# Decode attention beside a gated MLP on one core: masking moved to ScalarE, the gMLP in three pieces, four quarters summed without a fold

## The chip, the core and the metric

The kernel runs on one core of a Trainium2 chip. Five engines work side by side and meet through semaphores: TensorE (PE; its weight loads are the row PEld), VectorE (DVE), ScalarE (ACT), GpSimd (POOL) and SyncE (SP), which here only issues loads. Sixteen DMA engines move data between the chip's memory and the core's buffer. The metric is the device time of one launch in microseconds, as the median over runs; a profiled execution beside them gives the trace.

## The reference

Two blocks read the same normalized input and are added to it:

```python
xn = _layernorm(x, axis=-1)
return x + _A_ref(xn, A_k_cache, A_v_cache, A_wq, A_wo) + _B_ref(xn, B_w_in, B_w_sp, B_b_sp, B_w_out)
```

Block A is attention of one new position against a cache: batch 4, 32 heads, 4096 cached positions, head width 128, model width 640, all bf16.

```python
q = (x @ wq).reshape(B, Sq, Hq, Dh)          # one query per head
scores = einsum('bhqd,bhkd->bhqk', q, k) * Dh ** (-0.5)
p = _softmax(scores, axis=-1)
o = einsum('bhqk,bhkd->bhqd', p, v)
return o.reshape(B, Sq, Hq * Dh) @ wo
```

Block B is a small gated MLP (gMLP): `z = gelu(xn @ w_in)`, 1728 columns; its second half is layer-normalized, scaled by the single number `w_sp`, shifted by `b_sp`, and multiplied with the first half; the product goes through `w_out`.

K and V are 134 MB each, and every byte is used once.

## The kernel before

**Tiles.** The 32 heads are cut in 4 groups of 8, and with 4 batches that makes 16 tiles (`NT`), each 8 heads of one batch. In a tile, 16 partitions hold one head, and every partition holds 256 positions of 128 numbers. A K tile is 8 MB and a V tile as much, loaded in two halves (units). The ring in the core's buffer has five units: a pair for the K tile in work, a pair for the next, and a single one (`SOLO`); V halves take the places that K tiles and earlier V halves leave. The gMLP's weights lie in the single unit at the start.

**Loads.** All are issued from SyncE's queue, in the order of a plan made ahead (`plan_k`, `plan_v`, `load_wo`): K of tile i+2 after both V halves of tile i, and a slice of `wo` after tiles 0, 4 and 8. `pump()` issues the next load as soon as, in program order, the unit's holder is marked `used`; on the chip the queue then waits for the holder's last reader. The queue is in order: a load that waits for its place holds all behind it.

**One tile** (`for i in range(NT)`), its K in four quarters of 64 positions per partition:
- `product` (L495, VectorE): the quarter times the query, in place, 128x8192 bf16.
- `fold` (L504, VectorE): the upper 64 of each 128 products added to the lower 64.
- `sums` (L513, TensorE): 8 matmuls with the identity add the 64 columns up to 8 per position, into PSUM (`s_ps`, two buffers).
- `row_sums` (L527, VectorE) reduces the 8 to a score, one quarter behind: it comes after the next quarter's product.
- After the four: `lane_max` (L536 VectorE, L538 ScalarE, L540 TensorE), then `exps`: the maximum (L546, VectorE) and the exponential on ScalarE (L550), which gives `p`, 128x256 bf16.
- `deal` (L561): `p` is spread to `p_m`, where each position has 8 columns, one for each head, and all but the own head's are zeros (`hmask`). Two GpSimd instructions of 128x1024 for a tile; in the last tile one of the two is VectorE's. `p_m` has two buffers, for even and odd tiles.
- `blocks` (L575, TensorE): probabilities times V, 32 matmuls for each half. The first half of tile i-1 stands in tile i behind the sums of its first quarter, the second behind those of its third, followed by `gather` (L589 ScalarE, L593 TensorE). The last two tiles have an order of their own: in tile 14 the first half of 13 comes behind the fourth quarter, and in tile 15 four of these stages follow its quarters. Tile 14's `exps` and `deal` stand in tile 15 behind its first fold.

The order on TensorE, VectorE, ScalarE and SyncE is the program's own; GpSimd's and what stands before the loop is placed by a scheduler.

**The gMLP.** `gmlp_in` (L363): 70 matmuls behind the third quarter's sums of tile 0, into `zT`. `gmlp_out`, after tile 0's `exps` and `deal`: GELU on VectorE with tanh on ScalarE (L373 to L387), 14 matmuls for the layer norm's sums (L392), a chain of 1x4 and 1x8 instructions with a square root on ScalarE (L405 to L426), a broadcast matmul (L435, L439), three VectorE rows (L440 to L452) and the product with `w_out` (L456). Only then are the weights marked used and the second V half of tile 0, which takes their unit, may be issued. The two numbers `w_sp` and `b_sp` are loaded from ScalarE's queue at the start (L103, L104) and copied to fp32 on VectorE inside `gmlp_out` (L418, L420).

**After a group of four tiles**: sum of the exponentials (`group_den`, L617 on GpSimd, L624, L626), `group_norm`, `group_turn`, `group_pick` and the product with `wo` (`group_proj`, L671).

Of the kernel before, what the change touches and what calls it, by code (L numbers as in the profile page):

```python
# [20 lines left out]
def kernel(  # L21
# [14 lines left out]
    nc = tc.nc  # L36
# [316 lines left out]
    gm["ac"] = work.tile([1, 2 * Bsz], FP32, name="ac")  # L353
    gm["yT"] = work.tile([P, NFC, Bsz], BF16, name="yT")

    def gmlp_in():
        zT = gm["zT"] = ps_pv.tile([P, 2, NFC, Bsz], FP32, tag="pv", name="zT")
        for t in range(2):
            f1 = t * Fh + NFF * P
            w_t = w_in_sb[:, :, t * Fh : f1].rearrange("p c (f k) -> p c k f", k=NFF)  # L360
            for k in range(NFC):
                for c in range(DC):
# [6 lines left out]
                    )  # L369
    def gmlp_out():  # L370
        zT = gm["zT"]
# [15 lines left out]
        nc.vector.tensor_tensor(out=sq[:], in0=gz[:, 1, :, :], in1=gz[:, 1, :, :], op=ALU.mult)  # L387

        s_ps = ps_m.tile([1, 2 * Bsz], FP32, tag="m", name="ln_ps")
        for src, at in ((gz[:, 1, :, :], 0), (sq[:], Bsz)):  # L390
            for k in range(NFC):
# [6 lines left out]
                )  # L398
        st, ac = gm["st"], gm["ac"]
        mean_t = st[:, 0:Bsz]  # L400
# [15 lines left out]
        )  # L416
        wsp_t = work.tile([1, 1], FP32, name="wsp_t")
        nc.vector.tensor_copy(out=wsp_t[:], in_=wsp_bf[:])  # L418
        bsp_t = work.tile([1, 1], FP32, name="bsp_t")
        nc.vector.tensor_copy(out=bsp_t[:], in_=bsp_bf[:])  # L420
        nc.vector.reciprocal(out=rst_t, in_=rst_t)
# [71 lines left out]
    def product(i, q):  # L493
# [6 lines left out]
        )  # L500

    def fold(i, q):
        t = quarter(i, q)
        nc.vector.tensor_tensor(  # L504
            out=t[:, :, 0:HD2], in0=t[:, :, 0:HD2], in1=t[:, :, HD2:Dh], op=ALU.add
        )

    def sums(i, q):
        t = quarter(i, q)
        s = sums_ps[i, q] = ps_s.tile([P, QC, RW], FP32, name="s_ps")  # L510
        n = HD2 // RW
        for g in range(n):
            nc.tensor.matmul(  # L513
                out=s[:],
                lhsT=ident[:],
                rhs=t[:, :, g * RW : (g + 1) * RW],
                start=(g == 0),
                stop=(g == n - 1),
            )
        if q % 2:  # L520
            used.add(("k", i, q // 2))
            pump()
# [35 lines left out]

    def deal(i, part, engine):
        g0, g1 = part * UC // GC, (part + 1) * UC // GC  # L560
        engine.tensor_tensor(  # L561
            out=p_m[i % 2][:, g0:g1, :].rearrange("p g (c h) -> p g c h", h=HT),
            in0=probs[i][:, part * UC : (part + 1) * UC]
            .rearrange("p (g c) -> p g c", c=GC)[:, :, :, None]
            .to_broadcast([P, UC // GC, GC, HT]),
            in1=hmask_bf[:, None, None, :].to_broadcast([P, UC // GC, GC, HT]),
            op=ALU.mult,
        )
# [113 lines left out]
    with tc.manual_schedule(engines={E.PE, E.DVE, E.Activation, E.SP}):  # L682
# [3 lines left out]
        for i in range(NT):  # L686
            ends = i >= 1 and i % Bsz == 0
            late = i - 1 if i == LAST else None
            for q in range(NQ):
# [7 lines left out]
                if q == 0 and late is not None:  # L697
                    exps(late)
                    deal(late, 0, nc.gpsimd)
                    deal(late, 1, nc.gpsimd)  # L700
                sums(i, q)
                if i == 0 and q == 2:
                    gmlp_in()
                if i % Bsz == Bsz - 1 and q == 1 and i // Bsz + 1 < HG:
                    stage_q(i // Bsz + 1)
# [23 lines left out]
            if i != LAST - 1:  # L729
                row_sums(i, NQ - 1)  # L730
                lane_max(i)
                if ends:
                    group_pick(i // Bsz - 1)
                exps(i)
                deal(i, 0, nc.gpsimd)
                deal(i, 1, nc.vector if i == LAST else nc.gpsimd)
            if ends:
                group_proj(i // Bsz - 1)
            if i == 0:
                gmlp_out()  # L740
                used.add("w")
                pump()
        assert not loads
# [46 lines left out]
```

## Time and profile before

| | |
|---|---|
| runs, median (range), us | 672.07 (670.62 to 672.6) |
| the profiled execution, us | 668.78 |
| its span, us | 666.8 |
| PE, DVE, ACT, POOL busy, us | 313.4, 507.4, 34.3, 97.9 |
| product (L495), 64 rows, mean | 4.558 us |
| fold (L504), 64 rows, mean | 2.447 us |
| mask on GpSimd (L561), 31 rows, mean | 3.035 us |
| exp (L550), 16 rows, mean | 0.508 us |
| HBM read | 282.24 MB |

The span runs from the first to the last instruction of the program; the execution's own time has what lies around it. Busy times of different engines overlap. In a timeline row stand the start, the duration, engine, line and operation, the tile written and those read, and in brackets the idle time before it and what ended it. A row of SPq is SyncE's queue: "x2" merges two issues, with the time from the first's start to the second's end. A row of the waits has the waiting line, the one waited for, the sum, the count and the longest. In rows by stretches there are busy time and count for PE, PEld, DVE, ACT and POOL, the granted TensorE clock (1 is full), the share of the DMA engines' time, and GB/s.

### The profile page before, as it was taken

The page shows a single profiled execution, that of the slowest core. Times are in us where ns is not written, and L with a number is a line of the kernel's source. Part 1 is how long each engine was busy: PE and PEld are TensorE (multiplying, and loading weights), DVE is VectorE, ACT ScalarE, POOL GpSimd, SP SyncE. Part 2 cuts the span into 40 slices and gives each one's busy share as a digit, 9 for nine tenths or more (in the row PEclk, how much of TensorE's full clock was granted, in tenths as well). Part 3 has the DMA queues.
Part 4 walks back from the last instruction along what each step waited for, and adds up shares of the span by engine and source line. Part 5 has one row for each costly group of instructions (what it writes and reads, how often), then busy time and mean ns, then how long its engine had stood idle before and what let it go on. Part 6 is the DMA issues. An engine that isn't in the chain of part 4 may idle for free.

```text
span 666.8 us, 4747 instructions
## 1 busy us (share of the span) xinstructions
PE 313.4 (47%) x2033; PEld 127.2 (19%) x2033; DVE 507.4 (76%) x278; ACT 34.3 (5%) x82; POOL 97.9 (15%) x60
## 2 busy tenths in 40 slices
PE   0355461625544455453516545263553445535656
PEld 0113120211211112121212211121121111211223
DVE  2496986949595796977948499694958579799970
ACT  0002001000000000000000000000000000000000
POOL 2002002020200321302020050402010032120501
PEclk9755675777868577675767666777786756856786
DMA  9999899999999999999999999999999999999997
GB/s 376 438 451 408 361 448 436 437 413 468 412 432 447 409 448 416 462 430 415 442 420 450 423 417 460 419 440 421 453 417 429 449 421 374 440 411 436 410 424 288
DMA packets 9873, 282.56 MB, mean 424 GB/s; under 512 B 1040, under 2 KB 2428, under 8 KB 2812
## 3 DMA queue, kind: packets, MB, share of 16 engines
q1 hardware_dynamic: 9832, 282.25, 98.6%
q8 instruction: 16, 0.26, 0.1%
q14 instruction: 5, 0.04, 0.0%
q10 hardware_dynamic: 20, 0.01, 0.0%
HBM read 282.24 MB, written 0.01 MB: 423 GB/s over the span
## 4 chain that ended last, share of the span: by engine, by line
DMA 48%; DVE 34%; PE 17%; ACT 1%; issue 1%; SPq 0%; DVEq 0%; ACTq 0%
DMA ring<-in_A_k_cache_dram 41%; DVE ring L495 19%; DVE ring L504 11%; PE s_ps L513 10%; PE pv_acc L575 5%; DMA ring<-in_A_v_cache_dram 3%; DMA wo<-in_A_wo_dram 3%; DVE s_sb L527 2%; PE zT L363 1%; PE pv L593 0%; DVE gt L383 0%; PE max_ps L540 0%; DVE gz L386 0%; ACT pv_sb L589 0%; DVE m L536 0%
## 5 line engine op out<-in xcount | busy, mean ns | idle before, releaser
L495 DVE TENSOR_TENSOR ring<-ring,qbc 128x8192 bf16<-128x8192 bf16 x64 | 291.7, 4558 | 46.2 <-DMA ring<-in_A_k_cache_dram 46.2
L513 PE MATMUL s_ps<-ring,ident 128*128 128x512 bf16 x512 | 187.9, 533 | 284.0 <-DVE ring L504 284.0
L561 POOL TENSOR_TENSOR pm<-p,hmask_bf 128x1024 bf16<-128x1024 bf16 x31 | 93.5, 3035 | 548.6 <-ACT p L550 496.4
L504 DVE TENSOR_TENSOR ring<-ring 128x4096 bf16<-128x4096 bf16 x64 | 156.6, 2447 | 0.5
L513 PEld LDWEIGHTS <-ident 128*128 128x128 bf16 x512 | 63.9, 126 | 385.5 <-issue 320.0
L575 PE MATMUL pv_acc<-ring,pm 128*32 128x512 bf16 x1008 | 77.4, 462 | 0.9 <-DMA ring<-in_A_v_cache_dram 0.9
L527 DVE TENSOR_REDUCE s_sb<-s_ps 128x64 f32<-128x512 f32 x64 | 43.8, 684 | 43.3 <-PE s_ps L513 43.3
L575 PEld LDWEIGHTS <-pm 128*32 128x32 bf16 x1008 | 27.8, 114 | 58.4 <-issue 46.9
L589 ACT COPY pv_sb<-pv_acc 128x512 f32<-128x512 f32 x16 | 9.4, 586 | 364.4 <-PE pv_acc L575 364.4
L593 PE MATMUL pv<-sel,pv_sb 128*128 128x8 f32 x128 | 16.9, 259 | 11.9 <-ACT pv_sb L589 11.9
L626 DVE RECIPROCAL rden<-den 128x32 f32<-128x32 f32 x4 | 1.4, 358 | 26.1 <-PE den L624 26.1
L593 PEld LDWEIGHTS pv<-sel,pv_sb 128*128 128x128 f32 x128 | 15.5, 191 | 19.9 <-ACT pv_sb L589 19.9
L540 PE MATMUL max_ps<-lay,head_scale 128*128 128x16 f32 x32 | 7.0, 294 | 23.4 <-ACT lay L538 23.4
L538 ACT ACTIVATE lay<-lane_diag,m 128x16 f32<-128x16 f32 x16 | 4.9, 308 | 159.1 <-DVE m L536 159.1
L540 PEld LDWEIGHTS max_ps<-lay,head_scale 128*128 128x128 f32 x32 | 5.4, 211 | 30.6 <-ACT lay L538 30.6
L546 DVE TENSOR_REDUCE nb<-max_ps 128x1 f32<-128x16 f32 x16 | 2.8, 174 | 10.3 <-PE max_ps L540 10.1
L327 DVE CAST q_sb<-q_ps 128x512 bf16<-128x512 f32 x1 | 0.7, 692 | 12.9 <-PE q_ps L320 12.9
L320 PE MATMUL q_ps<-ring,xnT 128*32 128x512 bf16 x40 | 4.5, 630 | 10.6 <-DMA ring<-in_A_wq_dram 10.6
L550 ACT ACTIVATE p<-s_sb,nb 128x256 bf16<-128x256 f32 x16 | 8.1, 508 | 12.3 <-DVE nb L546 12.3
L536 DVE TENSOR_REDUCE m<-s_sb 128x1 f32<-128x256 f32 x16 | 6.7, 420 | 0.5
L631 DVE TENSOR_TENSOR o_n<-pv,rden 128x32 bf16<-128x32 f32 x4 | 0.7, 186 | 7.5 <-PE pv L605 7.5
L671 PE MATMUL out_ps<-wo,o_r 128*4 128x320 bf16 x48 | 6.0, 420 | 0.3 <-DVE o_r L658 0.2
(91 smaller groups left out, 72.2 us busy)
## 6 DMA issues: line engine op xcount, KB each, us to landing
ring<-in_A_v_cache_dram SPq DMA_DIRECT2D x31, 4096.0 KB, 30.8
ring<-in_A_k_cache_dram SPq DMA_DIRECT2D x2, 4096.0 KB, 34.0
ring<-in_A_wq_dram SPq DMA_DIRECT2D x1, 5120.0 KB, 15.6
wo<-in_A_wo_dram SPq DMA_DIRECT2D x3, 1280.0 KB, 16.9
ring<-in_B_w_in_dram SPq DMA_DIRECT2D x1, 2160.0 KB, 38.1
ring<-in_A_v_cache_dram SPq DMA_DIRECT2D x1, 2048.0 KB
ring<-in_A_v_cache_dram SPq DMA_DIRECT2D x1, 1024.0 KB
ring<-in_A_v_cache_dram SPq DMA_DIRECT2D x2, 512.0 KB, 25.8
```

The source lines that it names most:

```text
L363: nc.tensor.matmul(out=zT[: P if k < NFF else FT, t, k, :], lhsT=w_t[:, c, k, :] if k < NFF else w_in_sb[:, c, f1 : f1 + FT], rhs=xnT[:, c ...
L495: nc.vector.tensor_tensor(out=t, in0=t, in1=qbcs[i // Bsz][:, i % Bsz, None, :].to_broadcast([P, QC, Dh]), op=ALU.mult,)
L504: nc.vector.tensor_tensor(out=t[:, :, 0:HD2], in0=t[:, :, 0:HD2], in1=t[:, :, HD2:Dh], op=ALU.add)
L513: nc.tensor.matmul(out=s[:], lhsT=ident[:], rhs=t[:, :, g * RW : (g + 1) * RW], start=(g == 0), stop=(g == n - 1),)
L527: nc.vector.tensor_reduce(out=scores[i][:, q * QC : (q + 1) * QC], in_=sums_ps.pop((i, q))[:], axis=AX.X, op=ALU.add,)
L536: nc.vector.tensor_reduce(out=m1[:], in_=scores[i][:], axis=AX.X, op=ALU.max)
L540: nc.tensor.matmul(out=ps[:], lhsT=head_scale[:], rhs=d[:], start=True, stop=True)
L550: nc.scalar.activation(out=p[:], in_=scores.pop(i)[:], func=ACT.Exp, bias=nb[:], scale=scale_qk, accum_out=acc[hg % NACC][:, b : b + 1],)
L561: engine.tensor_tensor(out=p_m[i % 2][:, g0:g1, :].rearrange("p g (c h) -> p g c h", h=HT), in0=probs[i][:, part * UC : (part + 1) * UC] . ...
L575: nc.tensor.matmul(out=pv_acc[g * CW : (g + 1) * CW, :], lhsT=pm[:, (part * UC + c) // GC, :], rhs=v_nat[:, c : c + GC, :].rearrange("p c ...
L589: nc.scalar.copy(out=pv_sb[:], in_=pv_acc[:])
L593: nc.tensor.matmul(out=pvs[hg][:, :, b], lhsT=pv_sb[:, k * Dh : (k + 1) * Dh], rhs=sel[:, k, :], start=(k == 0), stop=stop and k == GC - 1,)
```

## The change

1. `deal` runs on ScalarE, as 8 activations for a tile, one for each head: a copy of `p` (128x256) scaled by that head's mask column, written to every eighth column of `p_m`. In the last tile both parts are VectorE's (`deal_part`). GpSimd has no part in it any more.
2. `gmlp_out` is cut in three. The GELU (`gmlp_gelu`) stands behind the sums of tile 0's fourth quarter, the layer norm's sums and root (`gmlp_stats`) and the rest (`gmlp_out`) behind tile 0's `lane_max`, before its `exps`. The copies of `w_sp` and `b_sp` move ahead of the loop; the scheduler puts them on VectorE among the first instructions, between the statistics of x and the reciprocal of its root.
3. In tiles 14 and 15 the first and the third quarter are not folded, and their sums take 16 matmuls over all 128 columns.

```diff
+    wsp_t = work.tile([1, 1], FP32, name="wsp_t")
+    nc.vector.tensor_copy(out=wsp_t[:], in_=wsp_bf[:])
+    bsp_t = work.tile([1, 1], FP32, name="bsp_t")
+    nc.vector.tensor_copy(out=bsp_t[:], in_=bsp_bf[:])
...
-    def gmlp_out():
+    def gmlp_gelu():
...
+    def gmlp_stats():
+        gz, sq = gm["gz"], gm["sq"]
         s_ps = ps_m.tile([1, 2 * Bsz], FP32, tag="m", name="ln_ps")
...
+    def gmlp_out():
+        gz, sq, st, ac = (gm[n] for n in ("gz", "sq", "st", "ac"))
...
+    def wide(i, q):
+        return i >= NT - 2 and q % 2 == 0
+
     def fold(i, q):
+        if wide(i, q):
+            return
...
-        n = HD2 // RW
+        n = (Dh if wide(i, q) else HD2) // RW
...
-    def deal(i, part, engine):
+    def deal(i):
+        by_head = p_m[i % 2][:].rearrange("p g (c h) -> p h (g c)", h=HT)
+        for h in range(HT):
+            nc.scalar.activation(
+                out=by_head[:, h, :],
+                in_=probs[i][:],
+                func=ACT.Copy,
+                scale=hmask[:, h : h + 1],
+            )
+
+    def deal_part(i, part):
         g0, g1 = part * UC // GC, (part + 1) * UC // GC
-        engine.tensor_tensor(
+        nc.vector.tensor_tensor(
...
                 if q == 0 and late is not None:
                     exps(late)
-                    deal(late, 0, nc.gpsimd)
-                    deal(late, 1, nc.gpsimd)
+                    deal(late)
                 sums(i, q)
                 if i == 0 and q == 2:
                     gmlp_in()
+                elif i == 0 and q == 3:
+                    gmlp_gelu()
...
+                if i == 0:
+                    gmlp_stats()
+                    gmlp_out()
+                    used.add("w")
+                    pump()
                 exps(i)
-                deal(i, 0, nc.gpsimd)
-                deal(i, 1, nc.vector if i == LAST else nc.gpsimd)
+                if i == LAST:
+                    deal_part(i, 0)
+                    deal_part(i, 1)
+                else:
+                    deal(i)
             if ends:
                 group_proj(i // Bsz - 1)
-            if i == 0:
-                gmlp_out()
-                used.add("w")
-                pump()
```

## The prediction

> **What bounds the kernel now.** I read the shares and the DMA rows of the page first, then the DMA rate by stretches of time, then SyncE's queue and its waits, and last the VectorE and GpSimd rows around the places where the rate falls.
>
> ```profile
> DMA  9999899999999999999999999999999999999997
> ...
> q1 hardware_dynamic: 9832, 282.25, 98.6%
> ```
>
> SyncE's one queue moves 282.25 MB and its packets fill 98.6% of the 16 engines' time, against 76% for VectorE and 47% for TensorE. So time can be won only where this queue runs empty. The next view is the rate in four stretches (last two columns: DMA share, GB/s).
>
> ```profile
> 65.00:75.00 10.00, 3.47 (x44) 2.12 (x45) 7.76 (x16) 0.46 (x2) 0.21 (x1) 0.50 0.91 368
> 555.00:565.00 10.00, 6.78 (x42) 2.14 (x41) 10.00 (x4) 0.00 (x0) 0.00 (x0) 0.71 0.80 318
> 615.00:625.00 10.00, 7.33 (x83) 3.47 (x83) 9.96 (x8) 1.50 (x4) 4.87 (x1) 0.98 0.92 372
> 100.00:540.00 440.00, 201.01 (x1244) 79.20 (x1243) 337.91 (x164) 20.26 (x51) 61.07 (x25) 0.70 1.00 433
> ```
>
> For 440 us the rate is 433 GB/s flat. Three stretches fall short, by 10 x (1 - rate/433) = 1.50, 2.66 and 1.41 us, 5.6 in all. These rows count a packet where it starts; I also spread each packet record of the trace over its own duration and set the bytes against 432.35 GB/s (its slope from 76 to 554 us). That gives 2.08, 2.36 and 0.96 us, 5.40 in all, and at most 0.2 in any other ten microseconds. I use these. With 2.86 lost at the start, 282.25 MB / 432.35 = 652.8, and some 5.3 after 655 us, the 666.8 is accounted for within 0.5.
>
> What leaves the queue empty is in SyncE's rows, its waits, and VectorE's and GpSimd's rows (start, us, work).
>
> ```profile
> 43.63 28.37 SPq L139 DMA_DIRECT2D ring<-in_A_v_cache_dram  x2
> 72.06 0.42 SPq L149 DMA_DIRECT2D wo<-in_A_wo_dram  x1
> ...
> 558.45 19.13 SPq L131 DMA_DIRECT2D ring<-in_A_k_cache_dram  x2
> ```
> ```profile
> SPq L139 <- PE out_ps L456: 27.6, 1, 27.6
> ```
> ```profile
> 506.36 2.29 DVE L504 TENSOR_TENSOR ring<-ring 128x4096 bf16<-128x4096 bf16 x1
> ...
> 548.32 3.86 DVE L504 TENSOR_TENSOR ring<-ring 128x4096 bf16<-128x4096 bf16 x1
> 552.11 6.11 DVE L495 TENSOR_TENSOR ring<-ring,qbc 128x8192 bf16<-128x8192 bf16 x1
> ```
> ```profile
> 544.73 9.21 POOL L561 TENSOR_TENSOR pm<-p,hmask_bf 128x1024 bf16<-128x1024 bf16 x2 [43.97 <-ACT p L550]
> ```
>
> The first hole: the second V half of tile 0 waits 27.6 us for the gMLP's last product (L456), because it takes the weights' place, and is issued only at 71.68. The second: K tile 14, issued at 558.45, waits for the PV matmuls of V half (12, 0), which follow tile 13's first product, fold and sums; that fold took 3.86 us instead of 2.29, inside GpSimd's 9.21 us. The third: V half (14, 0), issued at 617.21, waits for the PV matmuls of (13, 0), behind the whole of tile 14. By the packet records the bytes issued earlier ended 0.95, 1.02 and 2.41 us after these issues. Adding what was lost, a load must stand in the queue 3.0, 3.4 and 3.4 us ahead of the end; the next narrowest, K tile 15 with 3.71 and K tile 11 with 4.26, lost nothing.
>
> **The change part by part.** *gMLP earlier.* Before, the path is: tile 0's s_ps ends 57.9, row sum, maximum, lay and max_ps to 60.06, then the GELU chain from 60.27 to the ln_ps matmuls at 65.42, then 6.26 us to the issue at 71.68. The GELU rows (L373 to L387) now stand behind fold 3, which ends at 54.25, while zT ends at 54.26. Their six short rows are 0.1 to 0.25 us each, tanh 0.25, and L383 and L386, 1.90 and 1.84 us in GpSimd's stretch, should fall to the 0.2 of their neighbours: some 2 us, done by 56.5, under VectorE's 3.66 us wait for s_ps until 57.91. Without that cover they would cost their 2 us. The ln_ps matmuls follow max_ps at 60.1, and with the same 6.26 us the V half is issued at 66.4: 72.63 - 66.4 = 6.2 us ahead, well over 3.4. **First hole: -2.08 us.** The table load for the square root (1.28) fits after lay (59.40) and before the root at some 61.6. Behind this VectorE reads tile 0's maximum at 64.4, ScalarE loads the exp table (1.28), and the masked probabilities are there by 70, while the PV matmuls need them at 64.4 + 4.42 + 2.28 + 3.57 = 74.7: 5 us of cover. K tile 1 has landed at about 62.6. No load changes its place in SyncE's queue, here or later.
>
> *The two scalar copies at the start.* They now stand between the layer-norm statistics of x (end 3.86) and the reciprocal. Their two-byte loads end in the packet records at 5.75 and 8.78, their last markers at 7.27 and 10.30, one packet of the wq load between each. VectorE so stalls from 3.9 to about 10.6, and behind it wait xn, the constants and xnT, ready at some 14 instead of 7.6. The q projection starts with the wq load at 16.41: 2.4 us of cover, cost nothing. Were the loads behind all of wq, q would come 3.5 us later, at 26.5, against K's first landing at 26.05: half a microsecond, which the first hole's 2.8 us of spare lead takes.
>
> *Masking on ScalarE.* 15 x 8 activations of 128x256, bf16, with strided output, and 31 GpSimd rows go. The trace has no such activation. The nearest is exp (L550), the same shape with a per-partition operand: 0.508 us. From below: L538, 16 columns, 0.308; from above: GpSimd's contended pair, 9.21 / 8 = 1.15. I take 0.51, so 4.1 us a tile, on an engine that is 5% busy. It must be done when the PV matmuls come: 4.42 + 2.28 + 3.57 = 10.3 us after the tile's first product starts, and exp ends 0.65 after it where no K load is awaited. So even 1.15 x 8 + 0.65 = 9.9 fits; cost nothing. ScalarE's next work (pv_sb, q rows) comes 20 us later, but for tile 15, where pv_sb of tile 13 waits for the masking of 14, some 11 us into a tile whose next sums come at 14.
>
> What it gives: tile 13's fold goes from 3.86 to 2.28, K tile 14 is issued 1.58 us earlier relative to everything before it, and its lead becomes 2.60 of the 3.0 to 3.4 needed. **Second hole: -1.58 us**, with 0.8 left; bounds 1.0 and 2.36, since PV there took 2.65 us at half clock, and 1.87 in tile 9 at full clock. The other long folds and products stand before issues with over 4 us of lead, or before K waits: nothing.
>
> *Two unfolded quarters in tiles 14 and 15.* Each takes a 2.28 us fold away and adds 8 matmuls, 3.57 us at half clock and 1.89 at full. At half clock tile 14 runs, from its K landing: product to 4.4, 16 matmuls to 11.6, row sum 12.3 (VectorE waits for it; fold 1 and product 2 are queued behind), fold 14.6, sums 18.1; product 2 to 18.9, its 16 matmuls 26.1, row sum 26.8, fold 29.0, sums 32.6, PV 34.5. Before it was 617.2 - 581.5 = 35.7, 2 of which were GpSimd's (4.84 and 3.86 for product and fold). So the change of sums alone costs 0.8 at half clock, at full clock it gains some 4; with GpSimd gone the V half leads by 2.41 + 1.2 = 3.6 or more. **Third hole: -0.96 us.** In tile 15 everything waits for V halves from DMA, and the chain ends with the last wo load, 1.6 us of matmuls and the output, all unchanged. Masking tile 15 as two VectorE rows (2 x 1.23) ends 0.5 before GpSimd's part did.
>
> **Sum.** 2.08 + 1.58 + 0.96 = 4.6 us: span 666.8 to 662.2, and the profiled execution's own time 668.78 to 664.2. That execution lies 3.29 under the median of the runs, 672.07; I carry the difference over: **667.5 us**.
>
> One rule of the Trainium skill would give more. The page "SBUF — State Buffer", section "The DMA setup-cost knee", says that a DMA pays a fixed cost of about 2 us whatever its size. By that, an estimate, a lead of 2.60 us would be enough and the second hole would close whole, for the 666.7 us of the first rival below. The trace does not agree: K tile 14 and the V half (0, 1) fit 3.0 to 3.4, and V half (14, 0) lost 0.96 with a lead of 2.41.
>
> **Rivals.** *All three holes close* (chance 0.18). If PV of (12, 0) runs at full clock (1.87 as in tile 9, not 2.65), K tile 14 leads by 3.4: 5.4 us, **666.7**. For: the clock came 1.5 us too late there before. Against: it was half clock in tile 5 too (2.48).
>
> *Only the first closes* (0.15). Something that I have at nothing (the 0.8 of the unfolded sums, a clock that stays low) eats the later leads: 2.1 us, **670.0**. For: both leads have only tenths to spare.
>
> *Hidden anyway* (0.10). The holes belong to the profiled execution, and the timed ones are bound by a slower stream: **672.1**. For: they are 3.3 us longer. Against: the waits are structural.
>
> *The other side: strided masking is slow* (0.11). At d us each, masking passes the PV matmuls in tiles 1, 5, 9 and 13, which await no K load, when 8d > 9.6, d > 1.2. K tile 14 has no lead to spare and loses x = 8(d - 1.2); K tiles 6 and 10 have about 2.7 (4.4 and 4.6, plus 1.58, less 3.4) and lose x - 2.7 each. The gain is eaten at 3x - 5.4 = 4.6, d = 1.62; at 1.8 it is 672.07 - 4.64 + 9.0 = **676.4**. For: no row has such a stride. Against: it takes three times the exp row.
>
> **How the numbers follow.** My case has 0.46. 0.3% of 672 is 2.0 us, about what a measurement of this kernel can tell from no change, as the three runs spread over 2.0. Faster holds 0.46 and 0.18 nearly whole and half of the 0.15: 0.69; slower is the 0.11; the rest, 0.20, is within. The low end is all holes closed less the runs' lower spread of 1.45, 665.3; the high end is the hidden case, 672.1, beyond which lie slow masking and half of that case. My own case alone spans 666.5 to 668.7.
>
> **What would show it.** Right: 65 to 75 and 615 to 625 us at 433 GB/s, the V half issued near 66, folds all at 2.3, a small dip before K tile 14's issue, which stands near 555 us. Wrong: masking rows over 1.2 us, PV matmuls waiting for ScalarE, a late q projection, a new dip elsewhere, or dips closed and the end not moved.

## The result and the profile after

| | before | after |
|---|---|---|
| runs side by side, median (range, runs), us | 671.27 (670.18 to 672.6, 6) | 664.5 (663.34 to 666.26, 6) |
| profiled execution, its span, us | 668.78, 666.8 | 663.34, 661.4 |
| DVE, ACT, POOL busy, us | 507.4, 34.3, 97.9 | 476.9, 175.1, 5.6 |
| product, fold, mean, us | 4.558, 2.447 | 4.415, 2.282 |

Medians and ranges here and below leave out six runs that lie clearly above the others of their kernel: 691.92 of `e_nomask`, 684.19 of `c_shadow`, 689.1 of `d_fours_warm`, 1448.24 of `f_shadow_early`, and 692.65 and 683.61 of the kernel before.

The ratio is 0.99, 95% interval 0.9881 to 0.9919: faster by 6.8 us, where 4.6 were forecast. The page first, its DMA slices and SyncE's queue:

```profile
DMA  9999999999999999999999999999999999999997
...
q1 hardware_dynamic: 9832, 282.25, 99.1%
```

It was 98.6% with a slice at 8. The same four stretches as before (the last columns are the granted clock, the DMA share and GB/s):

```profile
65.00:75.00 10.00, 4.90 (x32) 1.64 (x32) 9.96 (x4) 8.92 (x8) 0.00 (x0) 0.56 1.02 439
555.00:565.00 10.00, 4.27 (x14) 1.62 (x14) 10.00 (x5) 0.00 (x0) 0.00 (x0) 0.85 0.96 408
615.00:625.00 10.00, 8.16 (x48) 3.90 (x48) 5.49 (x3) 4.28 (x5) 0.00 (x0) 0.58 1.04 449
100.00:540.00 440.00, 196.85 (x1250) 78.36 (x1250) 325.62 (x162) 117.60 (x133) 0.72 (x3) 0.71 1.00 433
```

The steady rate is 433 GB/s as before. The first and the third hole are gone, of the second a rest is left. Spread over the packet records, with the 432.35 GB/s of the prediction, 0.56 us are lost from 545 to 575 us (2.38 before), 0.44 of them in the ten from 555 on, at most 0.3 in any other ten between 10 and 655, and 2.70 at the start (2.86 before). SyncE's queue (start, duration, "x2" for two issues) and its wait for the gMLP:

```profile
42.97 22.69 SPq L139 DMA_DIRECT2D ring<-in_A_v_cache_dram  x2
65.71 0.42 SPq L149 DMA_DIRECT2D wo<-in_A_wo_dram  x1
...
553.79 0.33 SPq L131 DMA_DIRECT2D ring<-in_A_k_cache_dram  x1
```
```profile
SPq L139 <- PE out_ps L464: 21.9, 1, 21.9
```

The V half in the weights' place is issued at 65.33 (42.97 + 22.69 less its own 0.33) instead of 71.68, K tile 14 at 553.79 instead of 558.45. The work that releases K tile 14, tile 13's first quarter, in the timeline:

```profile
541.73 0.51 ACT L563 ACTIVATE p<-s_sb,nb 128x256 bf16<-128x256 f32 x1 [0.97 <-DVE nb L559]
542.37 9.41 ACT L575 ACTIVATE pm<-p,hmask 128x256 bf16<-128x256 bf16 x8
546.00 2.29 DVE L517 TENSOR_TENSOR ring<-ring 128x4096 bf16<-128x4096 bf16 x1
548.35 3.52 PE L526 MATMUL s_ps<-ring,ident 128*128 128x512 bf16 x8 [4.62 <-DVE ring L517]
551.83 1.91 PE L598 MATMUL pv_acc<-ring,pm 128*32 128x512 bf16 x32
```

The fold is back at 2.29. The masking takes 9.41 us, not 4.1, and ends at 551.78, 0.05 before the PV matmuls (L598) start. Tile 13's sums, at half clock, end at 551.87. Two conditions of the same matmuls so come true within 0.1 us. And the masking by itself, in the rows by line (busy, mean ns):

```profile
L575 ACT ACTIVATE pm<-p,hmask 128x256 bf16<-128x256 bf16 x120 | 140.8, 1604 | 0.5
```

One record is 1.60 us long, and the next starts 1.13 after it (the median over all 15 tiles), as records of neighbours overlap. A tile's eight take 9.41 / 8 = 1.18 each.

### The profile page after: what moved, and what is told of

It is laid out like the page before. It is cut to its first block, busy times and chain, and to the rows that moved or that the text cites. A ratio compares the mean times of both kernels' runs of the same rounds, so it can differ in the third digit from the quotient of the medians.

```text
span 661.4 us, 4848 instructions
## 1 busy us (share of the span) xinstructions
PE 310.3 (47%) x2065; PEld 128.8 (19%) x2065; DVE 476.9 (72%) x275; ACT 175.1 (26%) x202; POOL 5.6 (1%) x29
## 4 chain that ended last, share of the span: by engine, by line
DMA 50%; DVE 30%; PE 15%; ACT 4%; issue 1%; SPq 0%; DVEq 0%
DMA ring<-in_A_k_cache_dram 43%; DVE ring L503 19%; PE s_ps L526 9%; DVE ring L517 9%; PE pv_acc L598 4%; DMA ring<-in_A_v_cache_dram 4%; DMA wo<-in_A_wo_dram 3%; ACT pm L575 3%; DVE s_sb L540 2%; PE pv L616 0%; DVE m L549 0%; PE max_ps L553 0%; ACT pv_sb L612 0%; PE out_ps L694 0%; ACT L563 0%
## 5 line engine op out<-in xcount | busy, mean ns | idle before, releaser
L503 DVE TENSOR_TENSOR ring<-ring,qbc 128x8192 bf16<-128x8192 bf16 x64 | 282.5, 4415 | 65.2 <-DMA ring<-in_A_k_cache_dram 65.2
L575 ACT ACTIVATE pm<-p,hmask 128x256 bf16<-128x256 bf16 x120 | 140.8, 1604 | 0.5
L526 PEld LDWEIGHTS <-ident 128*128 128x128 bf16 x544 | 65.3, 122 | 382.4 <-issue 290.6
L517 DVE TENSOR_TENSOR ring<-ring 128x4096 bf16<-128x4096 bf16 x60 | 136.9, 2282 | 0.5
L598 PE MATMUL pv_acc<-ring,pm 128*32 128x512 bf16 x1008 | 75.5, 452 | 7.9 <-DMA ring<-in_A_v_cache_dram 7.8
L598 PEld LDWEIGHTS <-pm 128*32 128x32 bf16 x1008 | 27.8, 111 | 62.6 <-issue 46.2
L384 ACT ACTIVATE gt<-gw 128x56 f32<-128x56 f32 x1 | 0.2, 249 | 31.2 <-DVE gw L383 31.2
L640 POOL TENSOR_TENSOR own_sum<-acc,hmask 128x32 f32<-128x32 f32 x4 | 2.0, 500 | 627.4 <-ACT p L563 627.4
```

The lines of the kernel that those rows point to most:

```text
L503: nc.vector.tensor_tensor(out=t, in0=t, in1=qbcs[i // Bsz][:, i % Bsz, None, :].to_broadcast([P, QC, Dh]), op=ALU.mult,)
L517: nc.vector.tensor_tensor(out=t[:, :, 0:HD2], in0=t[:, :, 0:HD2], in1=t[:, :, HD2:Dh], op=ALU.add)
L526: nc.tensor.matmul(out=s[:], lhsT=ident[:], rhs=t[:, :, g * RW : (g + 1) * RW], start=(g == 0), stop=(g == n - 1),)
L575: nc.scalar.activation(out=by_head[:, h, :], in_=probs[i][:], func=ACT.Copy, scale=hmask[:, h : h + 1],)
L598: nc.tensor.matmul(out=pv_acc[g * CW : (g + 1) * CW, :], lhsT=pm[:, (part * UC + c) // GC, :], rhs=v_nat[:, c : c + GC, :].rearrange("p c ...
```

## The experiments

Three numbers of each profile are used: the *lead* of a load (when the bytes issued earlier ended, less the time of its issue; from the packet records, as in the prediction), the time lost from 545 to 575 us, where K tile 14 stands, and the median of the runs, with the ratio to runs of the kernel before on the same chip. The kernel before had 670.97, 670.51, 671.29, 670.16 and 671.1 beside the five groups. Where the first packets of the next load overlap the last ones of an earlier, a lead is good to some 0.5 us. V(0,1) is the V half that takes the weights' place, K14 is K tile 14, V(14,0) the first V half of tile 14.

| kernel | lead of V(0,1), K14, V(14,0), us | lost 545 to 575, us | median (range), us | ratio, 95% interval |
|---|---|---|---|---|
| before | 0.95, 1.02, 2.41 | 2.38 | 671.27 (670.18 to 672.6) | |
| after | 6.85, 3.39, 6.94 | 0.56 | 664.5 (663.34 to 666.26) | 0.9881 to 0.9919 |
| e_again | 6.84, 2.87, 5.58 | 0.97 | 664.7 (663.76 to 667.26) | 0.9863 to 0.9924 |
| e_nogmlp | -4.68, 2.69, 6.63 | 1.20 | 672.86 (670.95 to 674.44) | 0.9996 to 1.0037 |
| e_nomask | 10.36, 1.78, 6.51 | 1.83 | 669.36 (665.87 to 674.88) | 0.9928 to 0.9992 |
| e_nowide | 6.02, 3.51, 4.06 | 0.63 | 664.4 (663.59 to 666.55) | 0.986 to 0.9919 |
| b_before_warm | 1.54, 3.22, 2.73 | 0.54 | 670.81 (669.04 to 675.61) | 0.9956 to 1.0023 |
| b_nomask2 | 6.50, 0.78, 6.32 | 2.89 | 666.58 (one run) | |
| c_warm | 6.20, 3.54, 5.96 | 0.64 | 664.49 (663.75 to 666.45) | 0.9874 to 0.9932 |
| c_mask10 | 6.32, 0.43, 6.58 | 2.42 | 668.26 (665.6 to 672.05) | 0.9928 to 0.997 |
| c_flat | 6.04, 1.82, 6.30 | 1.69 | 664.65 (664.21 to 665.1) | 0.9876 to 0.9923 |
| c_shadow | 9.08, 1.92, 7.12 | 1.58 | 666.27 (665.33 to 668.58) | 0.9905 to 0.9961 |
| d_again | 6.59, 3.22, 6.38 | 0.79 | 664.66 (663.94 to 665.04) | 0.9903 to 0.9931 |
| d_fours | 5.78, 3.81, 7.02 | 0.34 | 665.57 (664.62 to 667.89) | 0.9924 to 0.9957 |
| d_fours_warm | 6.49, 4.90, 6.45 | 0.13 | 663.22 (662.93 to 665.5) | 0.9891 to 0.9924 |
| d_shadow_late | 7.08, 1.29, 5.82 | 2.14 | 667.5 (666.41 to 668.29) | 0.9949 to 0.9976 |

**The parts undone, one at a time.** `e_again` is the changed kernel once more.

> The changed kernel once more, beside the three others. Theory V (the timed executions scatter because holes open and close with the state of TensorE's clock): spans between 661.4 and 664.4, the profile with second hole between 0 and 1.5 us and all else within 0.3 of the first profile. Rival F (a fixed part around the span makes the timed runs longer): the profile's holes are those of the first within 0.1, and time less span is larger in the longer runs.

It gave 664.7. Its profile lost 0.97 us behind K tile 14 where the first lost 0.56, so one profile tells that term to some 0.4. Time less span is 1.7 to 1.9 us in all six runs, the longest too, so what makes a run longer lies inside the span (rival F fails).

`e_nogmlp` puts the gMLP back in one stretch behind tile 0's `exps` and masking:

```diff
-                elif i == 0 and q == 3:
-                    gmlp_gelu()
...
-                if i == 0:
-                    gmlp_stats()
-                    gmlp_out()
-                    used.add("w")
-                    pump()
                 exps(i)
...
+            if i == 0:
+                gmlp_gelu()
+                gmlp_stats()
+                gmlp_out()
+                used.add("w")
+                pump()
```

> The changed kernel with the gMLP back in one stretch behind tile 0's masking (the two scalar copies stay early). Theory H (the time is the load stream plus the holes in which SyncE's queue is empty): ScalarE now masks tile 0 for 9.4 us before it comes to the tanh, so the V half (0, 1) is issued at about 78 instead of 65.3, 6 us after the queue ran out; the first hole is 8 to 10 us, 673 to 675 us in all. Rival O (each part of the change is worth its own hole whatever the others do): the old hole of 2.1 comes back, 666.6.

The whole gain went, 8.2 us against `e_again`, four times what the first hole had cost. Its timeline shows why:

```profile
61.07 9.34 ACT L575 ACTIVATE pm<-p,hmask 128x256 bf16<-128x256 bf16 x8
69.92 0.53 ACT L384 ACTIVATE gt<-gw 128x56 f32<-128x56 f32 x1
...
70.48 0.19 DVE L387 TENSOR_SCALAR gt<-gt 128x56 f32<-128x56 f32 x1 [9.58 <-ACT gt L384]
...
77.32 0.33 SPq L139 DMA_DIRECT2D ring<-in_A_v_cache_dram  x1
```

The GELU's tanh (L384) stands behind eight masking activations, VectorE waits 9.58 us for it, and the V half is issued at 77.32. The rate falls to 250 and 272 GB/s in the two stretches from 65 to 85 us, 7.8 us lost. So the parts don't add up one by one. With the masking on GpSimd the gMLP's new place closes the first hole by itself (`b_nomask2` below, where V(0,1) leads by 6.50); with the masking on ScalarE the old place costs 7.8 us.

`e_nomask` (and `b_nomask2`, the same kernel for another profile) gives the masking back to GpSimd, with the two other parts kept:

```diff
-    def deal(i):
...
+    def deal(i, part, engine):
...
-                    deal(i)
+                deal(i, 0, nc.gpsimd)
+                deal(i, 1, nc.vector if i == LAST else nc.gpsimd)
```

> The changed kernel with the masking back on GpSimd. Theory H: the first hole stays closed; GpSimd's contention makes tile 13's fold 3.9 us again, K tile 14's lead falls by 1.6 to about 1.8 and the second hole is 1.6 to 2; the third stays closed, since without folds the quarters of tile 14 give GpSimd less to fight with: 666 to 666.5. Rival: the 9.4 us that masking takes on ScalarE holds back the PV matmuls as much as GpSimd did, and nothing changes, 664.5.

> The changed kernel with masking on GpSimd, for a profile without the slow stretch of packets that hit the first. V: first hole closed, second 1.6 to 2.5 us (lead 0.8 to 1.8), and K tile 15, with a lead of 3.0 in the first profile, loses 0.3 to 1 too: 666 to 669. S: second hole 1.6 alone, 665.5 to 666.5.

The ratio lies between before and after, at 0.996. In `b_nomask2` the first and the third hole are closed and the second is open (K tile 14 leads by 0.78, 2.89 lost): of the three holes only the second comes back with GpSimd's masking. The profile of `e_nomask` is no measure of it, since from some 42 to 81 us its packets took 1.39 us for 32 KB instead of 1.21. The runs of `e_nomask` fall in two bunches, four at 665.9 to 666.6 us and seven at 669.1 to 674.9. The first bunch is where `b_nomask2` (666.58) and its hole stand; the median of all, 4.7 us over `e_again`, is more than the hole explains. The one profile from the second bunch has the slow packets; that these make the other six too is not shown.

`e_nowide` folds all quarters:

```diff
     def wide(i, q):
-        return i >= NT - 2 and q % 2 == 0
+        return False
```

> The changed kernel with all quarters folded. Theory H: tile 14 takes 33.7 us from its K landing to the issue of V half (14, 0), against 31.0 with the unfolded quarters, and that half leads by over 4 us where 3.4 are needed: no hole, 664.5, no change that can be measured. Rival: the unfolded quarters closed the third hole, which comes back with up to 1 us, 665.5.

664.4 us, and V(14,0) still leads by 4.06. Unfolded, tile 14 is 2.9 us shorter (V(14,0) leads by 6.94), but the third hole is closed without it. In `b_nomask2` it is the other way round: GpSimd masks, the quarters are unfolded, and V(14,0) leads by 6.32. So either part alone closes the third hole, and beside the masking on ScalarE the unfolded quarters bring nothing that the runs can tell.

**What the second hole hangs on.** `b_before_warm` is the kernel before with 16 matmuls of ready data ahead of tile 13's first sums, into a buffer that the sums then overwrite. `c_warm` is the changed kernel with the same.

```diff
+    def warm(i):
+        s = ps_s.tile([P, QC, RW], FP32, name="s_ps")
+        for _ in range(WARM):
+            nc.tensor.matmul(
+                out=s[:].rearrange("p a b -> p (a b)"),
+                lhsT=ident[:],
+                rhs=qbcs[i // Bsz][:].rearrange("p b d -> p (b d)"),
+                start=True,
+                stop=True,
+            )
...
+                if i == NT - 3 and q == 0:
+                    warm(i)
                 sums(i, q)
```

> The kernel before with 16 more matmuls of 128x512 ahead of tile 13's first sums (their result is not used), so that TensorE runs when these come. If the second hole is made by the time from tile 13's first product to the PV matmuls of (12, 0), and half of TensorE's clock is part of it: sums at 1.9 in place of 3.57, PV 1.9 in place of 2.65, K tile 14 issued 1.7 to 2.4 earlier, second hole down to 0 to 0.7, time 1.7 to 2.3 less than before. Rival (the clock's state isn't set by this work, or K tile 14 waits for something else): no change.

> The changed kernel with 16 more matmuls of 128x512 ahead of tile 13's first sums (their result is not used). In the three profiles of such kernels K tile 14 leads by 3.4, 2.9 and 3.5 us and 0.4 to 0.8 us are lost there. Theory H: sums of tile 13's first quarter at 1.9 in place of 3.5, K tile 14 issued some 1 us earlier (masking then ends last, at 9.4 + 0.65 after the tile's start), hole below 0.2: 0.3 to 0.6 less, 664.0 to 664.3. Rival (masking on ScalarE is what K tile 14 waits for already): no change, 664.6, and the lead the same within 0.3.

In the kernel before, tile 13's sums and PV matmuls stood so:

```profile
552.24 3.57 PE L513 MATMUL s_ps<-ring,ident 128*128 128x512 bf16 x8 [6.18 <-DVE ring L504]
555.74 2.65 PE L575 MATMUL pv_acc<-ring,pm 128*32 128x512 bf16 x32
```

With the 16 matmuls its rows become:

```profile
545.78 4.24 PE L528 MATMUL s_ps<-qbc,ident 128*128 128x512 bf16 x16
548.11 3.86 DVE L505 TENSOR_TENSOR ring<-ring 128x4096 bf16<-128x4096 bf16 x1
...
552.03 1.89 PE L514 MATMUL s_ps<-ring,ident 128*128 128x512 bf16 x8 [2.01 <-DVE ring L505]
553.85 1.91 PE L587 MATMUL pv_acc<-ring,pm 128*32 128x512 bf16 x32
```

The sums take 1.89 us (3.57 at half clock), PV 1.91 (2.65), and with the fold as long as before K tile 14 leads by 3.22 and 0.54 us are lost. The mechanism of the second hole holds: it is the time from the tile's start to the last PV matmul. But the time didn't move (670.81). In the profile the next loads lost what this one won: 1.60 us at K tile 15, 1.31 at V(14,0), which before had lost nothing and 0.96. That profiled execution (671.91) is longer than the first one of before by 3.1 us, and this lies at its end: there tile 15's last sums take 3.35 us where they took 1.89, and after 650 us 8.9 us are lost instead of 5.3. With the changed kernel the same 16 matmuls moved the lead only to 3.54, because PV then waits for the masking:

```profile
542.38 9.46 ACT L587 ACTIVATE pm<-p,hmask 128x256 bf16<-128x256 bf16 x8
...
548.36 1.89 PE L527 MATMUL s_ps<-ring,ident 128*128 128x512 bf16 x8 [0.29 <-DVE ring L518]
...
551.90 1.91 PE L610 MATMUL pv_acc<-ring,pm 128*32 128x512 bf16 x32 [1.65 <-ACT pm L587]
```

The sums are done at 550.25, and PV stands 1.65 us idle until ScalarE's last activation.

**The price of the masking.** `c_mask10` does two of the eight activations twice; `c_flat` writes each activation's 256 values to neighbouring columns.

```diff
-        for h in range(HT):
+        for h in [*range(HT), 0, 1]:
```
```diff
-        by_head = p_m[i % 2][:].rearrange("p g (c h) -> p h (g c)", h=HT)
+        by_head = p_m[i % 2][:].rearrange("p g n -> p (g n)").rearrange("p (h s) -> p h s", h=HT)
```

> The changed kernel with ten masking activations a tile in place of eight (two are done twice). Masking takes 9.4 us a tile, 1.18 each, where the PV matmuls come 10.2 to 10.3 us after the tile's start. Theory C (masking is at the edge of its cover): it ends at 0.65 + 11.8 = 12.4, PV of (12, 0) is 2.1 to 2.3 late, K tile 14's lead falls to 1, and the second hole is 2.3 to 2.8; K tiles 6 and 10, with 5.7 to 6.6, lose nothing: 666.4 to 667. Rival (ScalarE has room, being 26% busy): no change.

> The changed kernel with each masking activation writing 256 neighbouring columns in place of every eighth one (the output is not the reference's). Theory W (the 1.60 us of one masking activation, three times exp's 0.51, come from the stride of the writing): each falls to 0.35 to 0.55 and a tile's masking to 3 to 4 us. Rival R (they come from the bf16 input or the per-partition scale): still 1.6. By theory H the time stays at 664.6, since tile 13's sums end as late as its masking; only tile 5's and tile 1's PV come 0.2 to 0.4 earlier.

With ten, the masking takes 11.71 us and passes the PV matmuls in the four tiles that await no K load. In the waits, with the sum, the count and the longest:

```profile
PE pv_acc L598 <- ACT pm L575: 10.1, 4, 2.9
```

K tile 14's lead falls to 0.43, 2.42 us are lost there and 0.9 at K tiles 6 and 10, and the time is 3.8 us over that of `c_warm` beside it. So the prediction's slow-side rival has its threshold right. The kernel as changed, with 9.41 us, stands on its edge. With neighbouring columns the eight take 3.31 us: the price is the step of the output, not ScalarE's arithmetic. The time stayed (664.65). In that profile tile 12 and 13 ran 0.95 us later, sums and PV at half clock (3.57 and 2.44), which the lead of 1.82 shows.

`c_shadow` leaves ScalarE's masking alone and lets GpSimd write the same values a second time, into a tile that nobody reads. `d_shadow_late` does so from tile 8 on, `f_shadow_early` in tiles 0 to 7, `f_shadow_zero` in tile 0.

```diff
+        for part in range(2 if i >= 8 else 0):
+            g0, g1 = part * UC // GC, (part + 1) * UC // GC
+            nc.gpsimd.tensor_tensor(
+                out=shadow[:, g0:g1, :].rearrange("p g (c h) -> p g c h", h=HT),
...
```

> The changed kernel, in which GpSimd also does its old masking of tiles 0 to 14, into a tile that nobody reads. Theory G (what the GpSimd masking cost was its contention with VectorE, not its own lateness): tile 13's first fold is 3.86 again, K tile 14's lead 0.8 to 1.8, second hole 1.6 to 2.8, as with the masking itself on GpSimd (666.58 in its undisturbed profile), and the timed runs scatter as widely as that kernel's (half of them over 669). Rival L (it was GpSimd's 9.2 us being late for the PV matmuls): K tile 14's lead as in the changed kernel, 664.6.

> As the changed kernel, but from tile 8 on GpSimd also writes the masked probabilities of each tile into a tile that nobody reads. Theory G (GpSimd's work slows VectorE): folds of 3.8 and products of 4.6 us or more appear from about 330 us on, K tile 14's lead falls under 2.6 us and 0.8 to 2.4 us are lost there; nothing changes in tiles 0 to 7. Theory P (the slow packets from 42 us on belong to GpSimd's masking in the early tiles): no stretch of packets over 1.30 us ahead of 300 us; time 665.0 to 667.0 with a narrow scatter, under 3 us between the runs but for a slow one. Rival P0 (they belong to the kernel as loaded, or to chance): packets of 1.35 us or more from 42 us on again, in the profile, and scatter over 3 us in the times.

Both bring the second hole back: 1.58 and 2.14 us are lost there. Tile 13 with the late copy:

```profile
542.35 9.40 ACT L576 ACTIVATE pm<-p,hmask 128x256 bf16<-128x256 bf16 x8
542.46 9.14 POOL L584 TENSOR_TENSOR shadow<-p,hmask_bf 128x1024 bf16<-128x1024 bf16 x2 [44.04 <-ACT p L564]
545.98 3.87 DVE L518 TENSOR_TENSOR ring<-ring 128x4096 bf16<-128x4096 bf16 x1
549.77 6.11 DVE L504 TENSOR_TENSOR ring<-ring,qbc 128x8192 bf16<-128x8192 bf16 x1
...
556.02 20.32 SPq L131 DMA_DIRECT2D ring<-in_A_k_cache_dram  x2
```

Nobody waits for GpSimd, yet the fold is 1.59 us longer than its 2.28 and the next product 1.69 longer than its 4.42. K tile 14 leads by 1.29; 2.14 us are lost there and 0.92 at K tile 15. The median is 2.84 us over `d_again` beside it (2.5 by the spans). `c_shadow`, with the copy in all tiles from 0 on, is only 1.6 us over the 664.66 of the changed kernel's 17 runs, and its runs reach 668.58, where half were expected over 669. So GpSimd's mere work, on an engine off every path, costs 1.6 to 2.8 us; the 4.7 us of `e_nomask` are not explained by it.

The order of these rows also says how. GpSimd's first instruction is issued at 542.46, while a product runs until 545.95; then the fold stands 1.59 us; then the second product stands 1.69. Taken in turns, a whole instruction at a time, 3.49 (to the product's end) + 1.59 + 2.28 (the fold) + 1.69 make 9.05 of GpSimd's 9.14 us. The Trainium skill, page "SBUF — State Buffer", section "Who interferes with whom", says that a VectorE instruction with two inputs in the buffer contends with a GpSimd instruction that reads it, over a shared port pair that is an exclusive lock. The trace agrees: the fold and the second product have two such inputs.

**Both limits of K tile 14 taken away.** In `d_fours` the columns of `p_m` stand in another order, so that each activation writes four neighbours and skips 28; `d_fours_warm` adds the 16 matmuls. `d_again` is the changed kernel beside them.

```diff
-        by_head = p_m[i % 2][:].rearrange("p g (c h) -> p h (g c)", h=HT)
+        by_head = p_m[i % 2][:].rearrange("p g (h c) -> p h g c", h=HT)
...
-                out=by_head[:, h, :],
-                in_=probs[i][:],
+                out=by_head[:, h],
+                in_=probs[i][:].rearrange("p (g c) -> p g c", c=GC),
...
-                rhs=pm[:, (part * UC + c) // GC, c % GC * HT : (c % GC + 1) * HT],
+                rhs=pm[:, (part * UC + c) // GC, :].rearrange("p (h c) -> p h c", h=HT)[:, :, c % GC],
```

> The changed kernel once more, beside the three others: 664.0 to 665.2, K tile 14's lead 2.8 to 3.4 us with 0.4 to 0.8 lost, packets of 1.21 us throughout. Theory P0 would let it show a stretch of 1.35 us packets in one profile out of two; theory P would not.

> The masked columns stand in another order: each masking activation writes four neighbouring columns and then skips 28, instead of every eighth. Theory M (K tile 14 waits for ScalarE's masking, and its cost is the stride of its output): the activation falls from 1.60 us to between 0.5 and 0.9, the masking of tile 13 ends at least 3 us before its sums. The sums of tile 13 then set the PV matmuls: at half clock (3.57) K tile 14's lead stays at 2.8 to 3.5 us with 0.3 to 0.8 lost, at full clock it is 4.5 or more with nothing lost. Time 663.8 to 664.8. Rival (the cost is the number of activations, not how they write): 1.4 us or more for each, lead and time as in the changed kernel, 664.5. Rival C (PV matmuls that read every fourth column cost more): PV of 32 matmuls over 2.9 us, time above 665.5.

> The same order of columns, and 16 matmuls whose result nobody reads ahead of tile 13's first sums. Theory M together with the clock: sums 1.9 and PV 1.9 us, masking done long before, K tile 14's lead over 4.5 us, nothing lost there, no stretch with a loss over 0.2 us between 30 and 650 us; time 663.6 to 664.4, that is 0.2 to 0.8 under the changed kernel. Theory S (something else holds K tile 14 back): the lead stays under 3.6 us and 0.4 or more is lost, as with the 16 matmuls alone (3.54 and 0.49).

The masking of `d_fours` by itself (minimum, median, maximum in ns):

```profile
L575 ACT ACTIVATE pm<-p,hmask x120: 491/492/510, 65.6 to 612.5; 128x256 bf16<-128x256 bf16 x120
```

0.49 us, a third of the changed kernel's, and as in `c_flat`. Runs of four are enough. K tile 14's lead went from 3.22 (`d_again`) to 3.81 only, the sums at half clock holding it; with the matmuls too it is 4.90:

```profile
542.17 3.30 ACT L587 ACTIVATE pm<-p,hmask 128x256 bf16<-128x256 bf16 x8
...
548.16 1.89 PE L527 MATMUL s_ps<-ring,ident 128*128 128x512 bf16 x8 [0.71 <-DVE ring L518]
549.97 1.91 PE L610 MATMUL pv_acc<-ring,pm 128*32 128x512 bf16 x32
551.93 20.81 SPq L132 DMA_DIRECT2D ring<-in_A_k_cache_dram  x2
```

So either limit alone, once gone, leaves the other (3.81, 3.54), and both gone close the hole (0.13 lost, no more than elsewhere). `d_fours_warm` has the fastest median of all kernels here, 663.22 against 664.66, but the intervals of the two ratios overlap, so they are not told apart. `d_fours` alone has a median 0.9 us over `d_again`, again with intervals that overlap. Only its rival C had a time above 665.5, and that rival's sign, PV matmuls over 2.9 us, isn't there: the halves take 2.33 us in the median (2.21 in the changed kernel). Its profile won 0.45 us at K tile 14 and lost 0.43 at K tile 15, where `d_again` lost nothing. The rest stands at the end of the timeline, of `d_fours_warm`, then of the changed kernel, then of `f_shadow_zero` (below), which has the old order of columns:

```profile
639.95 3.47 PE L527 MATMUL s_ps<-ring,ident 128*128 128x512 bf16 x8
...
648.21 5.31 PE L610 MATMUL pv_acc<-ring,pm 128*32 128x512 bf16 x48
```
```profile
645.66 3.60 PE L598 MATMUL pv_acc<-ring,pm 128*32 128x512 bf16 x32
...
649.77 1.47 PE L598 MATMUL pv_acc<-ring,pm 128*32 128x512 bf16 x16 [0.50 <-DMA ring<-in_A_v_cache_dram]
```
```profile
649.79 5.31 PE L609 MATMUL pv_acc<-ring,pm 128*32 128x512 bf16 x48
```

In the changed kernel the last PV matmuls wait for the last V bytes, until 649.77. In `d_fours_warm` tile 15's last sums are at half clock (3.47), its PV starts 2.55 us later, runs through without a wait and ends 2.3 us later (653.52 against 651.24), although the V bytes were there. In `d_fours` PV also starts late (648.46, ending at 653.75); there the sums are at full clock (1.89), and the PV matmuls ahead of them take 3.57 us where they took 1.91. The loads no longer set the end then: tile 15's own work does, some 2 us behind them, and what the hole gave is lost there. The order of columns is not what does it, since `f_shadow_zero` ends in the same way. Which matmuls of tile 15 run at half clock differs from one profile to the next; why was not found.

**Where the prediction's base lay.** `b_before1` and `b_before2` are the kernel before, each with one more profile.

> The kernel before, once more, for its profile. Two theories on why its timed runs (median 670.97) lie 2 us over its first profiled execution (668.78), while the changed kernel's lie 1 over its own. Theory V (holes vary): the leads of V half (0, 1), K tile 14 and V half (14, 0) fall with the state of TensorE's clock and GpSimd's contention; this profile shows the same three holes, 5.4 us and up to 2 more in them. Rival S (stream): the packets themselves are slower for some stretch, 1.39 us for 32 KB in place of 1.21 as seen once, in any kernel alike, and the holes are 5.4 within 0.4.

> The same once more. V: another sum of holes, with K tile 14's lead between 0 and 1.8 us. S: holes of 5.4 within 0.4, and whatever the time is over 668.8 lies in slower packets.

They took 669.68 and 670.34 (spans 667.7 and 668.2). The holes were there again: at K tile 14 2.46 and 2.30 us lost, at V(14,0) 0.96 and 1.00. But both had a stretch that the first profile hasn't. The 20 us from 45 on, in the first profile of before and in `b_before1`:

```profile
45.00:65.00 20.00, 11.28 (x88) 6.32 (x87) 14.81 (x14) 3.63 (x6) 3.54 (x2) 0.50 0.93 401
```
```profile
45.00:65.00 20.00, 11.27 (x88) 6.29 (x87) 14.81 (x14) 3.63 (x6) 3.66 (x2) 0.53 0.92 356
```

The same work on all engines, and 356 GB/s instead of 401: from some 42 us on, for 25 to 40 us, each 32 KB packet takes 1.36 us instead of 1.21. That loses 3 to 4 us, and hides the first hole (V(0,1) then leads by 3.6 and 4.4). Such a stretch stood in 4 of 7 profiles with GpSimd masking in all tiles (these two, `e_nomask`, and `c_shadow`, where it ends after some 20 us) and in none of 10 where ScalarE alone masks. In `before`, `after` and `b_nomask2` too the packets from 41 to 44 us are slow (1.30 to 1.36 us), but from 44 us on they are back at 1.21. Whether GpSimd's early tiles bring it was the last question.

> As the changed kernel, but in tiles 0 to 7 GpSimd also writes the masked probabilities into a tile that nobody reads. Theory P (slow packets in the early stream go with GpSimd's masking of the early tiles): packets of 1.35 us or more for tens of us from about 42 us on, or times that scatter by over 4 us; K tile 14's lead stays at 2.8 to 3.5 us as in the changed kernel, since no GpSimd work stands near it; time 664.7 to 668. Rival P0 (chance, or the kernel before as a whole): packets of 1.21 us throughout, times within 2.5 us of each other and 664.0 to 665.5.

> The same with tile 0 alone, two GpSimd instructions that would start near 68 us, when a slow stretch from 42 us on is well under way. Theory P in its narrow form (what stands around the first masking does it): the slow packets or the wide scatter are there as with tiles 0 to 7. Broad form (sustained GpSimd work): none, 664.0 to 665.3. Rival P0: none here and none with tiles 0 to 7.

It stays open. With tile 0 alone (665.85 us, 664.9 to 667.14, ratio 0.9902 to 0.9946) and with tile 8 and later the profiles show no slow packets. With tiles 0 to 7 the profiled execution was disturbed as a whole (1448 us, with matmuls several times their length) and can't be read; the other runs, 664.64 to 667.81, spread over 3.2 us, neither side's number, while their median, 666.79, lies in theory P's range and over rival P0's. The stretch also begins at 42 us, before any masking starts, which speaks against GpSimd's masking as its direct cause.

## Why the prediction was right or wrong

It had the sign, the three holes and what fills them right. It said 667.5 and the result is 664.5, under its own range. By its steps:

- *The bound.* Right. The steady rate is unchanged at 433 GB/s, and the span's 5.4 us come from the holes (2.08 + 1.82 + 0.96), 0.16 at the start, and 0.38 in what is left around them, most of it in a steady stretch that is faster by less than 0.1%.
- *gMLP earlier.* Right: V half forecast at 66.4, issued at 65.33, -2.08. What was missed is the tie to the masking: in the old order it is 7.8 us worse (`e_nogmlp`).
- *The two scalar copies.* Right. VectorE stalls at 7.72 and 10.75 as forecast, xnT is ready at 13.93, the q projection starts no later.
- *Masking on ScalarE.* Its price was mis-sized, 4.1 us a tile for 9.41 (1.18 each, against 0.51). That it costs nothing was right, but by 0.05 us, not by 6, and that was luck; in tile 0, where 5 us of cover were counted, the masking ends at 73.92 and the PV matmuls start at 73.97. The upper bound, "even 1.15 x 8 + 0.65", did hold room for it. The exp row had the shape but not the step of the output. The Trainium skill has a rule for that which the prediction didn't weigh: page "SBUF — State Buffer", section "Door 1: The DMA port swizzle" speaks of lines of 16 bytes, with a penalty for each access that goes to a new line. Every eighth bf16 column is a new line each time, 1604 ns; four neighbours, 492. The runs agree, and the page has no size for it.
- *The second hole.* Forecast -1.58 with 0.8 left, measured -1.82 with 0.56 (0.97 and 0.79 left in the two other profiles). The fold is back at 2.29 as said; the rest is that PV ran at full clock (1.91, not 2.65), the condition named in the rival where all holes close. That rival's lead of 3.4 came true (3.39), but not its end: the need was taken too short. At leads of 2.9 to 3.8 us 0.97 to 0.34 were still lost at K tile 14, at 4.90 nothing that stands out. It isn't one number either: K tile 15 lost nothing with 3.5 to 3.7 in four profiles.
- *Two unfolded quarters.* The third hole closed, as forecast. The working took half clock, by which the sums cost 0.8 us more; tile 14's two wide quarters took 5.71 and 3.61 us, not 7.2, and the tile became 2.9 us shorter. Either GpSimd's absence (`e_nowide`) or the quarters (`b_nomask2`) would have done.
- *The offset.* This step failed: "I carry the difference over", 3.29 us between one profiled execution and the median of three runs. For the changed kernel it is 1.16. Of the 3.0 us of the miss, 2.13 are this, and 0.86 the profiled execution (664.2 forecast, 663.34). The difference was no fixed term: among 78 runs of before beside all experiments (median 670.9), 5 were as fast as 668.78, and the median of the three, 672.07, lay over most. So 1.2 of the 3.29 us come from having three runs. The two other profiled executions of before stand 1.2 and 0.6 us under 670.9, the three of the changed kernel, 663.34, 663.76 and 663.94, 0.7 to 1.3 under the 664.66 of its 17 runs. With some 1.2 carried over the forecast would have been 665.4. The other 2.1 us of before may in part be the kernel's own, and lost by the change: slow packets stood in two of its three profiles, and in none of the changed kernel. What makes the runs differ by 1 to 3 us (slow packets, the clock in tile 15) is shown in part and not explained.
- *The rivals.* "Hidden anyway" and "strided masking is slow" didn't come true. The latter was near: two more activations for each tile cost 3.8 us. By luck the chip's 1.18 each stayed just under the 1.2 that it named.

## What to carry to other kernels

Before a profile's time is set against a median, count how its own executions scatter: here one profile and three runs differed by 3.3 us, more than the change's largest part. An engine off every path is not free: GpSimd's masking cost 1.6 to 2.8 us by standing in VectorE's way, and moving it paid although ScalarE took three times the time that its arithmetic needs. When two conditions of one wait end within 0.1 us, taking either away shows little; take both away, and then look for the next bound right behind them.

## What the runs showed of the hardware

- ScalarE, 256 bf16 columns written to every eighth column: 1604 ns (1.13 us from start to start); to neighbours, or in runs of four: 492 ns (0.40).
- Stretches of 20 to 40 us in which the packets of a load stream take 1.36 to 1.39 us for 32 KB instead of 1.21, with nothing changed on any engine.
- A load of 8 MB had to stand in the queue 3.4 to 4.2 us before the bytes ahead of it ended: at leads of 2.7 to 3.8 us at K tile 14 the stream still lost 1.2 to 0.34, and over the kernels of the table that lost there lead and loss add up to 3.4 to 4.2 (2.85 in `c_mask10`). At K tile 15 leads of 3.5 to 3.7 lost nothing.
- Behind 16 matmuls without use, 3.6 to 4.9 us of TensorE's time, tile 13's first sums took 1.89 us in three kernels, one profile each; without them they took 3.36 to 3.57. TensorE stood idle for 0.3 to 2.0 us before those sums with them, and for 4.6 to 6.2 without.
